# A gated-recurrence and star-ReLU kernel: a weight cast by its own DMA, a held-back weight load and an earlier logarithm

## The chip, the cores and the metric

The kernel runs on one core of one Trainium2 chip. A core has five engines with instruction streams of their own: PE (TensorE, matrix multiply), DVE (VectorE), ACT (ScalarE), POOL (GpSimd) and SP (SyncE, which here only issues DMAs). Each engine runs its instructions in the order in which they were written, and waits on semaphores for the others. The metric is the device time of one execution in microseconds, lower is better.

## The reference

Two steps in one kernel. The first is a gated linear recurrence over 768 steps, for 4 batches and 8 heads of 48 channels; the second is a feed-forward layer with a squared ReLU (here called the MoE work, after its inputs' names).

```python
for t in range(S):                       # S = 768, D = 48
    state = alpha[:, :, t, :, None] * state + einsum('bhd,bhe->bhde', k[:, :, t], v[:, :, t])
    y[:, :, t] = einsum('bhd,bhde->bhe', q[:, :, t], state)
x = y.transpose(0, 2, 1, 3).reshape(3072, 384)
h = x @ w_in                             # 384 x 2048
r = maximum(h, 0)
out = (s * (r * r) + b) @ w_out          # 2048 x 384
```

All inputs and the output are float32 in HBM.

## The kernel before

The 3072 tokens are worked through in 24 blocks of 128 (4 batches of 6 blocks). For each block `n`:

- `load(n)` (L121) issues four DMAs on SP: alpha, k, q and v, 192 KB each, in rows of 192 bytes. There are 8 buffers (`NLD`).
- `ln(n)` (L188) takes the logarithm of alpha on ACT. `vcast(n)` (L191) casts v to bf16 on POOL. `cum(n)` (L194) sums the logarithms over the block with a triangular matrix on PE, and ACT makes the exponentials `bi` and `b` of both signs.
- `qk(n)` (L225) multiplies k and q by these on DVE. `tr(n)` (L229) transposes both on PE, and DVE copies the result (`qkT`). `amat(n)` (L242) makes the attention matrix on PE, and DVE masks it (`am_a`, `am_b`).
- `yp(n)` (L262) makes y on PE: first the part from the state (it reads `sd`), then the part within the block (it reads `am` and the cast v), then the new addend of the state. ACT copies y out.
- `st(n)` (L329) updates the state: one DVE instruction (`t1`), then two halves of `sd` (L344) and `sc` (L348) on POOL.
- `xt(n)` (L314) transposes y on PE, and ACT writes it as x (`xd`).

The MoE work runs in groups: group 0 holds blocks 0 and 1, and each later group one block. `mp(g, u)` (L358) makes four (or two, for group 0) 128-column pieces of h, `rl` (L376) applies ReLU on ACT, `sq` (L384) squares on DVE, and `mm2(n, u)` (L394, called as `o`) multiplies a quarter of the result by w_out. `mr` is `mp` and `rl`; `busy(n)` (L177) is n matmuls whose result nobody reads.

The weights come in quarters. `load_w_in(i)` loads 512 columns of w_in (768 KB, rows of 2 KB) as float32 into `w_in_st`, and `cast_w_in` casts them to bf16, one or two of the three pieces on ACT and the others on DVE. `load_w_out` loads a quarter of w_out into `w_out_st`, and `cast_w_out` (`wout`) casts it, times s, on DVE, the second quarter on ACT. `w_in_st` is used again later for outputs of blocks 0 to 13 that wait for the bias.

No scheduler sets the order. The DMAs ahead of the loop are issued in the order in which they stand (L445 to L458): loads 0 to 3, four quarters of w_in, four of w_out, loads 4 to 7, all on SP. The work of the first blocks is a list written out by hand (L501 to L513); each entry is one call, and each engine gets its instructions in that order. The entries behind it have a number as their place, 8 per block, and are sorted by it (L548).

Of the kernel before, what the change touches and what calls it, by code (L numbers as in the profile page):

```python
# [10 lines left out]
AF = mybir.ActivationFunctionType  # L11
# [3 lines left out]
def kernel(  # L15
# [12 lines left out]
    nc = tc.nc  # L28
# [8 lines left out]
    NJ = d_ff // 128  # L37
    KT = d_model // 128
# [5 lines left out]
    NLD = 8  # L44
# [59 lines left out]
    w_in_st = sb.tile([128, KT, d_ff], FP32, name="w_in_st")  # L104
    w_in_bf = sb.tile([128, KT, d_ff], BF16, name="w_in_bf")
    w_out_st = sb.tile([128, NJ, d_model], FP32, name="w_out_st")
# [10 lines left out]
    def src(t, n):  # L117
        b, c = n // NCH, n % NCH
        return t[b, :, c * C : (c + 1) * C, :].rearrange("h s d -> s h d")

    def load(n):  # L121
        if n < NBLK:
            for dst, t in ((al_sb, alpha), (k_sb, k), (q_sb, q), (v_sb, v)):
                nc.sync.dma_start(out=dst[n % NLD], in_=src(t, n))

    def load_w_in(i):
        cols = slice(i * d_ff // 4, (i + 1) * d_ff // 4)
        nc.sync.dma_start(
            out=w_in_st[:, :, cols], in_=moe_w_in[:, cols].rearrange("(t r) f -> r t f", t=KT)
        )  # L130

    def load_w_out(j0, j1):
        nc.sync.dma_start(
            out=w_out_st[:, j0:j1],
            in_=moe_w_out[128 * j0 : 128 * j1, :].rearrange("(j r) m -> r j m", r=128),
        )

    def cast_w_in(c0, c1, act=1):
        for kk in range(act):
            nc.scalar.activation(out=w_in_bf[:, kk, c0:c1], in_=w_in_st[:, kk, c0:c1], func=AF.Copy)  # L140
        for kk in range(act, KT):
            nc.vector.tensor_copy(out=w_in_bf[:, kk, c0:c1], in_=w_in_st[:, kk, c0:c1])

    def cast_w_out(j0, j1, act):
        if not act:
# [304 lines left out]
    quarter = d_ff // 4  # L450
    load(2)
    load(3)
    for i in range(4):
        load_w_in(i)
    for j in range(0, NJ, 4):
        load_w_out(j, j + 4)
    for n in range(4, NLD):
        load(n)  # L458
    make_upper_triangular(nc, U_bf, 1.0, diag=True)
    for t in la_sb:  # L460
        nc.vector.memset(t, 0.0)
# [13 lines left out]
    def at(pos, fn, *args):  # L475
        events.append((pos, len(events), fn, args))
# [5 lines left out]
    def wout(i):  # L482
        cast_w_out(4 * i, 4 * i + 4, i == 1)

    def win(i):
        cast_w_in(i * quarter, (i + 1) * quarter, 2 if i == 0 else 1)

    def m(g, u):
        mp(g, u)
# [10 lines left out]

    for pos, what in enumerate(  # L501
        [
            (ln, 0), (vcast, 0), (cum, 0), (qk, 0), (spread,), (busy, 3), (tr, 0), (ln, 1), (busy, 1), (vcast, 1), (cum, 1), (amat, 0),
            (busy, 3), (yp, 0), (qk, 1), (st, 0), (busy, 1), (tr, 1), (xt, 0), (ln, 2), (busy, 2), (vcast, 2), (cum, 2), (amat, 1),
            (busy, 3), (yp, 1), (qk, 2), (st, 1), (busy, 1), (tr, 2), (xt, 1), (ln, 3), (busy, 2), (vcast, 3), (cum, 3), (amat, 2),
            (busy, 3), (yp, 2), (qk, 3), (st, 2), (busy, 1), (tr, 3), (xt, 2), (busy, 3), (amat, 3), (win, 0), (busy, 4), (yp, 3),
            (mr, 0, 0), (mr, 0, 1), (xt, 3), (mr, 1, 0), (win, 1), (sq, 0, 0), (mr, 0, 2), (mr, 0, 3), (mr, 1, 1), (win, 2), (sq, 0, 1),
            (sq, 1, 0), (mr, 2, 0), (mr, 2, 1), (win, 3), (st, 3), (sq, 0, 2), (sq, 0, 3), (mr, 0, 4), (mr, 0, 5), (wout, 0), (mr, 1, 2),
            (sq, 1, 1), (sq, 2, 0), (mr, 2, 2), (sq, 2, 1), (mr, 0, 6), (sq, 0, 4), (o, 0, 0), (wout, 1), (mr, 0, 7), (sq, 0, 5),
            (o, 1, 0), (mr, 1, 3), (sq, 1, 2), (o, 2, 0), (mr, 2, 3), (sq, 2, 2), (sq, 0, 6), (wout, 2), (sq, 0, 7), (o, 0, 1), (sq, 1, 3),  # L510
            (o, 1, 1), (sq, 2, 3), (ln, 4), (wout, 3), (o, 2, 1), (cum, 4), (o, 0, 2), (vcast, 4), (qk, 4), (o, 1, 2), (o, 2, 2), (colsum, 1),
            (o, 0, 3), (o, 1, 3), (tr, 4), (o, 2, 3), (o, 3, 0), (colsum, 2), (amat, 4),
        ]  # L513
    ):
        at(0.1 * pos, *what)
# [12 lines left out]
    for n in range(4, NBLK):  # L528
        p = 8 * n
        if n > 4:  # L530
            f = min((n - 5) / 3.0, 1.0)
            c, t, a = 9.0 + 5.8 * f, 5.8 + 5.0 * f, 3.4 + 4.5 * f
# [47 lines left out]
```

## Time and profile before

| | |
|---|---|
| three runs | 196.47, 197.56, 197.69 us, median 197.56 |
| the profiled execution | 196.55 us, its span 194.8 us |
| busy, of the span | PE 180.9 us (93%), DVE 150.5 (77%), ACT 119.5 (61%), POOL 61.4 (32%) |
| DMA queue of SP | 113422 packets, 29.94 MB, 74.3% of 16 engines |
| granted TensorE clock | 1.00 |

The page gives the span of one execution, measured by the profiler, and the busy time of each engine in it. Matmuls overlap, so a busy PE is not PE at its peak. Where a wait is shown, the profile names what ended last before the waiting instruction started. The difference of 1.75 us between the execution's time and its span lies outside the span.

### The profile page before, as it was taken

The page shows a single profiled execution, that of the slowest core. Times are in us where ns is not written, and L with a number is a line of the kernel's source. Part 1 is how long each engine was busy: PE and PEld are TensorE (multiplying, and loading weights), DVE is VectorE, ACT ScalarE, POOL GpSimd, SP SyncE. Part 2 cuts the span into 40 slices and gives each one's busy share as a digit, 9 for nine tenths or more (in the row PEclk, how much of TensorE's full clock was granted, in tenths as well). Part 3 has the DMA queues.
Part 4 walks back from the last instruction along what each step waited for, and adds up shares of the span by engine and source line. Part 5 has one row for each costly group of instructions (what it writes and reads, how often), then busy time and mean ns, then how long its engine had stood idle before and what let it go on. Part 6 is the DMA issues. An engine that isn't in the chain of part 4 may idle for free.

```text
span 194.8 us, 6003 instructions
## 1 busy us (share of the span) xinstructions
PE 180.9 (93%) x2389; PEld 143.3 (74%) x2391; DVE 150.5 (77%) x294; ACT 119.5 (61%) x245; POOL 61.4 (32%) x96
## 2 busy tenths in 40 slices
PE   1977879999999999999999999999999999999994
PEld 1544459866777788778878888888877877877783
DVE  5367778657687788888887996878988988998532
ACT  3344567953677666766677676775675566654640
POOL 5154404021310515624500641642401565352000
PEclk9999999999999999999999999999999999999999
DMA  6999999999996484484958448759886948433212
GB/s 126 188 185 190 359 388 371 233 192 188 186 156 108 71 155 88 80 150 82 173 91 162 83 85 162 131 80 198 165 175 149 216 117 166 128 120 121 84 40 81
DMA packets 113453, 30.31 MB, mean 156 GB/s; under 512 B 106627, under 2 KB 111890, under 8 KB 113426
## 3 DMA queue, kind: packets, MB, share of 16 engines
q1 hardware_dynamic: 113422, 29.94, 74.3%
q8 instruction: 18, 0.29, 0.7%
q14 instruction: 9, 0.07, 0.1%
q10 hardware_dynamic: 4, 0.00, 0.0%
HBM read 25.19 MB, written 4.74 MB: 154 GB/s over the span
## 4 chain that ended last, share of the span: by engine, by line
PE 80%; DVE 4%; ACT 3%; issue 1%; ACTq 0%
PE h_ps L365 29%; PE o_ps L403 28%; PE ct_ps L232 5%; PE a_ps L247 3%; PE a_ps L403 3%; PE y_ps L275 2%; ACT r_sb L379 2%; PE h_ps L317 2%; PE ct_ps L198 2%; PE a_ps L426 1%; PE p_ps L286 1%; PE y_ps L266 1%; DVE gt_all L386 1%; DVE w_out_bf L146 1%; DVE am_b L255 1%
## 5 line engine op out<-in xcount | busy, mean ns | idle before, releaser
L379 ACT ACTIVATE r_sb<-h_ps 128x512 bf16<-128x512 f32 x90 | 53.5, 597 | 35.5 <-PE h_ps L365 33.2
L365 PEld LDWEIGHTS <-w_in_bf 128*128 128x128 bf16 x1104 | 67.9, 98 | 8.0 <-ACT w_in_bf L140 1.4
L365 PE MATMUL h_ps<-xd_all,w_in_bf 128*128 128x128 bf16 (+1 forms) x1044 | 71.1, 221 | 0.1
L403 PE MATMUL o_ps<-w_out_bf,gt_all 128*128 128x384 bf16 x336 | 68.3, 326 | 0.1
L386 DVE TENSOR_TENSOR gt_all<-r_sb 128x512 bf16<-128x512 bf16 x96 | 45.1, 482 | 26.5 <-ACT r_sb L379 25.8
L344 POOL TENSOR_TENSOR sd_sb<-t_sb,blast 48x192 bf16<-48x192 f32 x40 | 20.1, 503 | 91.8 <-DVE t_sb L339 53.9
L403 PEld LDWEIGHTS <-gt_all 128*128 128x128 bf16 x368 | 32.6, 98 | 16.0
L192 POOL CAST v_bf<-v_sb 128x384 bf16<-128x384 f32 x24 | 17.0, 712 | 24.2 <-DMA v_sb<-in_v_dram 20.7
L348 POOL TENSOR_TENSOR sc_sb<-t_sb,blast 112x384 f32<-112x384 f32 x16 | 22.0, 1372 | 1.3
L323 ACT ACTIVATE xd_all<-h_ps 128x384 bf16<-128x384 bf16 x23 | 11.3, 491 | 15.6 <-PE h_ps L317 15.6
L237 DVE COPY qkT<-ct_ps 112x1024 bf16<-112x1024 bf16 x24 | 16.4, 683 | 4.5 <-PE ct_ps L232 3.0
L255 DVE TENSOR_TENSOR am_a<-a_ps,mask 128x512 bf16<-128x512 f32 x24 | 16.4, 683 | 4.2 <-PE a_ps L247 4.1
L226 DVE TENSOR_TENSOR kb_sb<-k_sb,bi_sb 128x384 bf16<-128x384 f32 x24 | 13.8, 574 | 4.5 <-ACT bi_sb L209 4.5
L255 DVE TENSOR_TENSOR am_b<-a_ps,mask 128x512 bf16<-128x512 f32 x24 | 16.3, 680 | 0.0
L227 DVE TENSOR_TENSOR qb_sb<-q_sb,b_sb 128x384 bf16<-128x384 f32 x24 | 16.0, 668 | 0.0
L293 ACT ACTIVATE y_bf<-y_ps 128x384 bf16<-128x384 f32 x24 | 11.7, 489 | 5.6 <-PE y_ps L275 5.6
L189 ACT ACTIVATE la_sb<-al_sb 128x384 bf16<-128x384 f32 x24 | 12.4, 516 | 3.9 <-DMA al_sb<-in_alpha_dram 3.9
L232 PEld LDWEIGHTS <-qb_sb 128*112 128x112 bf16 x96 | 8.3, 133 | 5.3 <-DVE qb_sb L227 4.1
L209 ACT ACTIVATE bi_sb<-ct_ps 128x384 f32<-128x384 f32 x20 | 9.7, 486 | 2.3 <-PE ct_ps L201 1.3
L232 PE MATMUL ct_ps<-ident,qb_sb 128*112 128x128 bf16 x96 | 9.9, 227 | 0.9 <-DVE qb_sb L227 0.9
L210 ACT ACTIVATE b_sb<-ct_ps 128x384 f32<-128x384 f32 x20 | 9.9, 495 | 0.0
L275 PE MATMUL y_ps<-v_bf,am_b 128*128 128x48 bf16 x96 | 8.1, 184 | 1.7 <-DVE am_b L255 1.7
(75 smaller groups left out, 200.9 us busy)
## 6 DMA issues: line engine op xcount, KB each, us to landing
al_sb<-in_alpha_dram SPq DMA_DIRECT2D x24, 192.0 KB, 4.1
k_sb<-in_k_dram SPq DMA_DIRECT2D x24, 192.0 KB, 4.0
q_sb<-in_q_dram SPq DMA_DIRECT2D x24, 192.0 KB, 4.4
v_sb<-in_v_dram SPq DMA_DIRECT2D x24, 192.0 KB, 5.2
w_in_st<-in_moe_w_in_dram SPq DMA_DIRECT2D x4, 768.0 KB
w_out_st<-in_moe_w_out_dram SPq DMA_DIRECT2D x4, 768.0 KB, 12.8
out_dram<-w_in_st SPq DMA_DIRECT2D x14, 192.0 KB, 2.0
out_dram<-out_sb SPq DMA_DIRECT2D x9, 192.0 KB
```

The lines of the kernel that those rows point to most:

```text
L192: nc.gpsimd.tensor_copy(out=v_bf[n % 3], in_=v_sb[n % NLD])
L226: nc.vector.tensor_tensor(out=kb_sb[n % 3][:, :, 0:48], in0=k_sb[n % NLD], in1=bi_sb[n % 2], op=ALU.mult)
L227: nc.vector.tensor_tensor(out=qb_sb[n % 2][:, :, 0:48], in0=q_sb[n % NLD], in1=b_sb[n % 3], op=ALU.mult)
L232: nc.tensor.transpose(out=t_ps[0:112, x, p, :], in_=t.rearrange("a h d -> a (h d)")[:, 128 * p : 128 * p + 112], identity=ident,)
L237: nc.vector.tensor_copy(out=qkT_sb[n % 2][0:112].rearrange("a x p t -> a (x p t)"), in_=t_ps[0:112].rearrange("a x p t -> a (x p t)"),)
L255: nc.vector.tensor_tensor(out=am_sb[e][n % 2], in0=a_ps[e], in1=mask4, op=ALU.mult)
L344: nc.gpsimd.tensor_tensor(out=sd[r, :, d], in0=t1_sb[r, :, d], in1=bl[r].to_broadcast([48, NP, 48]), op=ALU.mult)
L348: nc.gpsimd.tensor_tensor(out=sc_sb[0:112], in0=t1_sb[0:112], in1=bl[0:112].to_broadcast([112, NP, 96]), op=ALU.mult)
L365: nc.tensor.matmul(out=hp[:, jj * N : (jj + 1) * N], lhsT=w_in_bf[:, kk, 128 * j : 128 * (j + 1)], rhs=xd_sb[g][:, kk, 0:N], start=(kk == ...
L379: nc.scalar.activation(out=rs, in_=h_of.pop((g, u)), func=AF.Relu)
L386: nc.vector.tensor_tensor(out=gt_sb[g][:, u * 512 : (u + 1) * 512], in0=rs, in1=rs, op=ALU.mult)
L403: nc.tensor.matmul(out=op[:, 0:d_model], lhsT=gt_sb[g][:, j * N + t * C : j * N + (t + 1) * C], rhs=w_out_bf[:, j, :], start=(j == 0), sto ...
```

## The change

It has three parts. First, `load_w_in` writes straight into the bf16 tile `w_in_bf`: the DMA casts, and POOL issues it instead of SP. The casts on ACT and DVE (`cast_w_in`, `win`) go. Quarters 0 and 1 are issued after `vcast(2)`, quarters 2 and 3 after `vcast(3)`, in the list. Second, the loads of w_out and loads 4 to 7 are issued in a new entry `weights_out`, behind `sq(0, 0)`; ahead of them DVE writes one column of `w_out_st`, so the first w_out load has to wait for that write, and SP's later DMAs stand behind it. Third, the list is in another order: `ln(2)` stands ahead of `xt(0)` and `ln(3)` ahead of `xt(1)`, `amat(0)` ahead of `cum(1)`, the first MoE group `mr(0, 0)` ahead of `yp(3)`, six `busy` matmuls fewer, and `ln(4)`, `cum(4)` and `tr(4)` each a place or more earlier.

```diff
     def load_w_in(i):
         cols = slice(i * d_ff // 4, (i + 1) * d_ff // 4)
-        nc.sync.dma_start(
-            out=w_in_st[:, :, cols], in_=moe_w_in[:, cols].rearrange("(t r) f -> r t f", t=KT)
+        nc.gpsimd.dma_start(
+            out=w_in_bf[:, :, cols], in_=moe_w_in[:, cols].rearrange("(t r) f -> r t f", t=KT)
         )
...
-    def cast_w_in(c0, c1, act=1):
-        for kk in range(act):
-            nc.scalar.activation(out=w_in_bf[:, kk, c0:c1], in_=w_in_st[:, kk, c0:c1], func=AF.Copy)
-        for kk in range(act, KT):
-            nc.vector.tensor_copy(out=w_in_bf[:, kk, c0:c1], in_=w_in_st[:, kk, c0:c1])
...
     load(2)
     load(3)
-    for i in range(4):
-        load_w_in(i)
-    for j in range(0, NJ, 4):
-        load_w_out(j, j + 4)
-    for n in range(4, NLD):
-        load(n)
...
-    def win(i):
-        cast_w_in(i * quarter, (i + 1) * quarter, 2 if i == 0 else 1)
+    def weights_out():
+        nc.vector.memset(w_out_st[:, 0, 0:1], 0.0)
+        for j in range(0, NJ, 4):
+            load_w_out(j, j + 4)
+        for n in range(4, NLD):
+            load(n)
...
-            (ln, 0), (vcast, 0), (cum, 0), (qk, 0), (spread,), (busy, 3), (tr, 0), (ln, 1), (busy, 1), (vcast, 1), (cum, 1), (amat, 0),
-            (busy, 3), (yp, 0), (qk, 1), (st, 0), (busy, 1), (tr, 1), (xt, 0), (ln, 2), (busy, 2), (vcast, 2), (cum, 2), (amat, 1),
-            (busy, 3), (yp, 1), (qk, 2), (st, 1), (busy, 1), (tr, 2), (xt, 1), (ln, 3), (busy, 2), (vcast, 3), (cum, 3), (amat, 2),
-            (busy, 3), (yp, 2), (qk, 3), (st, 2), (busy, 1), (tr, 3), (xt, 2), (busy, 3), (amat, 3), (win, 0), (busy, 4), (yp, 3),
-            (mr, 0, 0), (mr, 0, 1), (xt, 3), (mr, 1, 0), (win, 1), (sq, 0, 0), (mr, 0, 2), (mr, 0, 3), (mr, 1, 1), (win, 2), (sq, 0, 1),
-            (sq, 1, 0), (mr, 2, 0), (mr, 2, 1), (win, 3), (st, 3), (sq, 0, 2), (sq, 0, 3), (mr, 0, 4), (mr, 0, 5), (wout, 0), (mr, 1, 2),
+            (ln, 0), (vcast, 0), (cum, 0), (qk, 0), (spread,), (busy, 2), (tr, 0), (ln, 1), (busy, 1), (vcast, 1), (amat, 0), (cum, 1),
+            (busy, 3), (yp, 0), (qk, 1), (st, 0), (busy, 1), (tr, 1), (ln, 2), (xt, 0), (vcast, 2), (load_w_in, 0), (load_w_in, 1), (cum, 2), (busy, 1), (amat, 1),
+            (busy, 3), (yp, 1), (qk, 2), (st, 1), (busy, 1), (tr, 2), (ln, 3), (xt, 1), (vcast, 3), (load_w_in, 2), (load_w_in, 3), (cum, 3), (busy, 1), (amat, 2),
+            (busy, 3), (yp, 2), (qk, 3), (st, 2), (busy, 1), (tr, 3), (xt, 2), (busy, 3),
+            (amat, 3), (mr, 0, 0), (busy, 1), (yp, 3), (mr, 0, 1), (sq, 0, 0), (weights_out,), (mr, 1, 0), (xt, 3), (st, 3), (sq, 0, 1), (mr, 0, 2),
+            (sq, 1, 0), (mr, 0, 3), (sq, 0, 2), (mr, 1, 1), (sq, 0, 3), (mr, 2, 0), (mr, 2, 1), (mr, 0, 4), (mr, 0, 5), (wout, 0), (mr, 1, 2),
...
```

The rest of the list differs only in the places of `ln(4)`, `cum(4)`, `wout(3)` and `tr(4)`.

More of the change, by code (lines that the diff above doesn't have):

```diff
@@ L509 @@
             (sq, 1, 1), (sq, 2, 0), (mr, 2, 2), (sq, 2, 1), (mr, 0, 6), (sq, 0, 4), (o, 0, 0), (wout, 1), (mr, 0, 7), (sq, 0, 5),
-            (o, 1, 0), (mr, 1, 3), (sq, 1, 2), (o, 2, 0), (mr, 2, 3), (sq, 2, 2), (sq, 0, 6), (wout, 2), (sq, 0, 7), (o, 0, 1), (sq, 1, 3),
-            (o, 1, 1), (sq, 2, 3), (ln, 4), (wout, 3), (o, 2, 1), (cum, 4), (o, 0, 2), (vcast, 4), (qk, 4), (o, 1, 2), (o, 2, 2), (colsum, 1),
-            (o, 0, 3), (o, 1, 3), (tr, 4), (o, 2, 3), (o, 3, 0), (colsum, 2), (amat, 4),
+            (o, 1, 0), (mr, 1, 3), (sq, 1, 2), (o, 2, 0), (mr, 2, 3), (sq, 2, 2), (sq, 0, 6), (ln, 4), (wout, 2), (sq, 0, 7), (o, 0, 1),
@@ L513 @@
+            (sq, 1, 3), (o, 1, 1), (sq, 2, 3), (cum, 4), (wout, 3), (o, 2, 1), (o, 0, 2), (vcast, 4), (qk, 4), (o, 1, 2), (o, 2, 2),
+            (colsum, 1), (o, 0, 3), (tr, 4), (o, 1, 3), (o, 2, 3), (o, 3, 0), (colsum, 2), (amat, 4),
         ]
```

## The prediction

> **What bounds the kernel now.** I read the page first: its busy row and its slices.
>
> ```profile
> span 194.8 us, 6003 instructions
> PE 180.9 (93%) x2389; PEld 143.3 (74%) x2391; DVE 150.5 (77%) x294; ACT 119.5 (61%) x245; POOL 61.4 (32%) x96
> ...
> PE   1977879999999999999999999999999999999994
> ...
> DMA  6999999999996484484958448759886948433212
> ```
>
> From about 44 us on, PE is full in every slice. A change ahead of that point moves the end by what it moves the start of that stretch, and nothing in this change reaches past block 4. So I looked at the first 45 us: first the busy time by stage (columns: stretch, sum, then PE, PEld, DVE, ACT, POOL busy, PE clock, DMA share, GB/s).
>
> ```profile
> 12.50:15.00 2.50, 1.89 (x22) 1.16 (x22) 1.02 (x2) 1.56 (x4) 1.83 (x3) 1.00 1.36 187
> ...
> 20.00:22.50 2.50, 1.73 (x24) 1.11 (x23) 2.50 (x5) 0.83 (x3) 0.50 (x1) 1.00 1.02 359
> ...
> 27.50:30.00 2.50, 1.26 (x18) 1.02 (x15) 2.40 (x8) 1.75 (x4) 0.00 (x0) 1.00 1.06 380
> ```
>
> Block inputs move at 187 GB/s, a block (768 KB) in some 4.2 us; weights move at about 370 GB/s, a quarter of w_in (768 KB) in 2.1 us. PE has a hole at 27.5 to 30 us. The timeline and the waits say what stands around it (start, length, engine, line).
>
> ```profile
> 15.09 0.99 SPq L124 DMA_DIRECT2D v_sb<-in_v_dram  x1
> 16.13 3.55 SPq L128 DMA_DIRECT2D w_in_st<-in_moe_w_in_dram  x4
> 17.94 0.49 ACT L323 ACTIVATE xd_all<-h_ps 128x384 bf16<-128x384 bf16 x1 [1.05 <-PE h_ps L317]
> 18.32 0.52 ACT L189 ACTIVATE la_sb<-al_sb 128x384 bf16<-128x384 f32 x1
> 18.89 0.32 PE L198 MATMUL h_ps<-la_sb,U_bf 128*128 128x384 bf16 x1 [0.56 <-ACT la_sb L189]
> 19.30 0.40 PE L247 MATMUL a_ps<-qkT 48*128 48x128 bf16 x8
> 20.75 0.50 POOL L192 CAST v_bf<-v_sb 128x384 bf16<-128x384 f32 x1 [1.13 <-DMA v_sb<-in_v_dram]
> 22.74 1.08 POOL L344 TENSOR_TENSOR sd_sb<-t_sb,blast 48x192 bf16<-48x192 f32 x2 [1.49 <-DVE t_sb L339]
> 24.82 0.34 PE L266 MATMUL y_ps<-sd_sb,qkT 112*128 112x96 bf16 x4
> 25.75 1.47 PE L365 MATMUL h_ps<-xd_all,w_in_bf 128*128 128x256 bf16 x12
> 29.30 0.83 PE L365 MATMUL a_ps<-xd_all,w_in_bf 128*128 128x256 bf16 x6 [1.24 <-ACT w_in_bf L140]
> 36.27 0.81 PE L403 MATMUL o_ps<-w_out_bf,gt_all 128*128 128x384 bf16 x4
> ```
>
> The reader should see two things. Until 25 us one chain runs from block to block: logarithm, cumulative sum, exponentials, products, transposes, attention matrix, `yp`. The MoE work of blocks 0 to 2 stands behind `yp(3)` on PE and starts at 25.9 us, though x of blocks 0 and 1 has been ready since 18.4. From there to the first `o(0,0)` at 36.27, PE also waits once 1.24 us for a w_in cast on ACT. No wait names the landing of w_in: the casts in the engines' order, not the transfer, are late.
>
> **The change part by part.**
>
> *Logarithm ahead of x.* For block 3, qkT of block 2 is complete at 18.46, but `amat(2)` starts at 19.30, since `cum(3)` (18.89) stands before it on PE and waits for `ln(3)` (18.32), which stands behind x of block 1 on ACT. y of block 1 leaves ACT at 16.89; alpha of block 1 landed at 8.24, so with 4.2 us a block those of blocks 2 and 3 land at 12.4 and 16.6. `ln(3)` can run at 16.9, and `cum(3)` no longer holds `amat(2)`: 0.84 us. `amat(1)` gains as much (14.23 against a qkT complete at 13.39). The swap of `cum(1)` and `amat(0)` gives up to 0.57 (9.23 against 8.66), most of which alpha of block 2 at 12.4 takes back. I take 1.6 in all: `amat(3)` at 22.0 instead of 23.62. Bounds: 0.3 (alpha late) to 2.2. The six `busy` matmuls taken out (0.21 us each) lie in PE's waits: nothing, with the clock at 1.00 in every slice; without such waits they would be worth 1.3.
>
> *w_in written as bf16 by its own DMA.* It removes 7 DVE casts of 0.42 (2.9 us) and 5 ACT casts of 0.62 (3.1 us). From the second MoE group (26.58) to `o(0,0)` (36.27) are 9.7 us; PE's own work there is 12 groups of 0.66 and `xt(3)` of 0.17, 8.1 us. So 1.6 us are waits, 1.24 of them at the cast. ACT keeps 0.6 us a group against PE's 0.66 and one w_out cast of 1.57, so I take 1.2; bounds 0.5 to 1.6.
>
> *The four issues on POOL.* No row of this trace shows a DMA that POOL issues. The nearest are SP's issues of the same transfers, 0.49 to 1.47 us each (3.55 for four); the longest bulk-weight issue is w_out's 2.63. I take 1.2 each, between SP's mean of 0.89 and its longest, because POOL is the slowest of these engines at comparable work (0.50 to 1.08 a step); bounds 0.5 to 2.63. Two stand between `vcast(2)` and `sd` of block 1, two between `vcast(3)` and `sd` of block 2. The first pair: `vcast(2)` at 15.64, so POOL is free at 18.5, `sd` done 19.6, just when `yp(2)` wants it. The second pair is on the path: `vcast(3)` can't start before v of block 3 has landed (20.75), then 0.5 + 2 x 1.2 + 1.08 gives `sd` at 24.7. So `yp(3)` waits on POOL at 24.8, no longer on the masks (`am` of block 3 done at 23.7). Most of the 1.6 us of the logarithm are hidden under this wait; of them remains that the first MoE group (0.66), which the new order puts before `yp(3)`, runs at 22.4 inside it.
>
> *The transfer.* Data of the first pair begins at about 18 (first issue done at 17.4; SP's first load, issued at 0.74, landed at 3.79 with 1.05 of moving, so some 2 us pass around the moving, part of them ahead of it), when load 3, whose last issue ended at 16.08, has its last packets under way. Landing after issue was 3.7 us for v of blocks 1 and 2, 4.7 for v of block 3, with w_in behind it already. I leave 20.75. Rate: 370 GB/s of reading as now (2.1 us a quarter); bounds 187 GB/s, the slowest steady rate here (4.2 us), and free.
>
> *w_out behind the small write.* The write stands behind `sq(0,0)` on DVE, at about 24.3, costs under 0.1 (0.06 for a 128x1 memset), and holds on SP the four w_out issues and the sixteen of loads 4 to 7. With w_in's second pair moving from 23.7, w_out 25.5 on, DMA has 12.6 us of weights to move: done at 36.3, the first w_out chunk at about 31 (its cast is wanted by 33.7), alpha of block 4 at 38.7. `cum(4)` is reached at 39.2, so the cover is half a microsecond; each later microsecond of the write then costs one.
>
> The sum: `yp(3)` at 24.8 takes 0.7 on PE, the second MoE group starts at 25.5 instead of 26.58: 1.1. Waits behind it: 1.2. Together 2.3 us of the profiled execution's 196.55: 194.25. The median shown is 197.56, 1.0 above that execution, so the median after would be 195.3.
>
> A rule weighed against this: the Trainium skill, DMA: Bandwidth & Descriptors (Queues, rings and completion order), says that every DMA engine takes turns packet by packet between the queues that have work. The trace, with nearly all on one queue, can't show it; v of block 3 was 1.0 us later when w_in stood behind it. By the rule the second queue's large packets go between load 3's small ones, and the sum would be that of the first rival.
>
> **The rivals.**
>
> 1. *Two queues share the engines and load 3 is late.* A packet of load 3 is 192 B (16.5 ns at 187 GB/s over 16 engines), a row of w_in 2 KB (87 ns at 370). If they alternate, v of block 3 lands only when the first pair has moved: 4.2 us on top of 19.8 (15.64 of block 2 and 4.2), 24.0 instead of 20.75. `yp(3)` follows to 28.05, and 3.25 - 2.3 makes 0.95 slower: 198.5. For: small packets, no slack on POOL. Against: most of load 3 has moved by 18 us.
>
> 2. *The casting transfer is slow* (the other side). Place: v of block 3, POOL's second pair, `sd`, `yp(3)`. At 187 GB/s the pair takes 8.4 us; shared with load 3, v lands up to 7 us after 19.8, at 26.8, `yp(3)` at 30.85: 6.05 - 2.3 = 3.75 slower, 201.3. It decides from v landing plus twice the issue beyond 25.5 (now 23.15): no gain from there, and the same point is passed by issues of 2.4 us each. For: no row has a casting transfer. Against: it writes half the bytes.
>
> 3. *Hidden anyway.* ACT's evacuations (16 of 0.60 beside PE's groups of 0.66) take the place of the casts, and POOL's wait eats the logarithm: 0.5 faster, 197.1. For: ACT had 2.2 to 2.5 of 2.5 us busy from 30 to 35. Against: the 1.24 us wait names the cast.
>
> 4. *Issues cost little* (0.5 each): `yp(3)` at 23.7 by the masks, 1.1 more gain and some of the waits: 193.9.
>
> **How the numbers follow.** Forecast 0.36 (its own range 194 to 196.5), rival 1 0.20, rival 2 0.22, rival 3 0.12, rival 4 0.10. About 1% (2 us) is what a measurement of this kernel tells from no change; the forecast lies just past that line, so some 0.30 of its 0.36 counts as faster. Faster 0.30 + 0.10 = 0.40. Same: 0.06 + rival 3's 0.12 + 0.13 of rival 1 = 0.31. Slower: 0.22 of rival 2 and 0.07 of rival 1 = 0.29. The range goes from 193.2 (rival 4 with all waits) to 200.8, short of the far end of rival 2.
>
> **What would show it.** Right: `ln(3)` at about 17, `amat(3)` at 22, POOL's two steps of about 1.2 us after `vcast(3)`, `sd` of block 2 ending just before `yp(3)`, the second MoE group at 25.5, no wait on w_in, `o(0,0)` at about 33.7, `cum(4)` by 39.5. Wrong: v of block 3 after 22, issues of over 2 us, a PE hole over 3 us ahead of `yp(3)`, ACT or PE waiting for alpha of block 4 beyond 40, or matmuls at half speed after the hole.

## The result and the profile after

The changed kernel takes 195.35 us (median, 195.03 to 196.52); the kernel before, run beside it, 197.14 (196.40 to 197.75). The ratio is 0.9928, with a 95% interval of 0.9902 to 0.9954: about 0.7% faster. The profiled execution of the changed kernel took 195.13 us, 1.42 less than that of before. The ratios here and below are worked out from the executions, two slow ones left out (one of e3, one of e6), and not from the medians.

First the page of the changed kernel: span, busy row, and the slices of PE and DMA.

```profile
span 193.4 us, 5976 instructions
PE 181.0 (94%) x2383; PEld 143.9 (74%) x2385; DVE 147.9 (76%) x288; ACT 117.6 (61%) x240; POOL 65.5 (34%) x100
...
PE   0898899979899999999999999999999999999993
...
DMA  6999999999996586482969656949794957433212
```

The span fell by 1.4 us at the same busy time of PE. From about 45 us on PE was full before and is full now; what changed lies ahead of that. The stretches of the changed kernel (sum, then PE, PEld, DVE, ACT, POOL busy, PE clock, DMA share, GB/s) show where:

```profile
27.50:30.00 2.50, 2.50 (x43) 2.44 (x42) 0.95 (x2) 2.27 (x5) 0.39 (x1) 1.00 0.97 260
...
37.50:40.00 2.50, 1.40 (x10) 0.74 (x9) 2.01 (x4) 1.08 (x2) 0.00 (x0) 1.00 0.89 174
```

The hole that stood at 27.5 to 30 us is filled. A new one stands at 37.5 to 40. The timeline of the changed kernel (start, length, engine, line; in brackets the idle time before and what ended it) gives the steps. `ln` is now L183, `cum` L192, `amat` L241, `yp` L260, `mp` L359, `o` L397.

```profile
16.73 0.52 ACT L183 ACTIVATE la_sb<-al_sb 128x384 bf16<-128x384 f32 x1
19.61 0.50 POOL L186 CAST v_bf<-v_sb 128x384 bf16<-128x384 f32 x1
20.07 1.57 POOL L128 DMA_DIRECT2D w_in_bf<-in_moe_w_in_dram  x2
21.67 1.10 POOL L338 TENSOR_TENSOR sd_sb<-t_sb,blast 48x192 bf16<-48x192 f32 x2
22.49 0.40 PE L241 MATMUL a_ps<-qkT 48*128 48x128 bf16 x8
23.70 0.34 PE L260 MATMUL y_ps<-sd_sb,qkT 112*128 112x96 bf16 x4
24.62 0.82 PE L359 MATMUL h_ps<-xd_all,w_in_bf 128*128 128x256 bf16 x6
24.69 0.06 DVE L474 MEMSET w_out_st<- 128x1 f32 x1
24.79 2.90 SPq L133 DMA_DIRECT2D w_out_st<-in_moe_w_out_dram  x4
33.30 0.82 PE L397 MATMUL o_ps<-w_out_bf,gt_all 128*128 128x384 bf16 x4 [0.22 <-DVE w_out_bf L140]
39.25 0.52 ACT L183 ACTIVATE la_sb<-al_sb 128x384 bf16<-128x384 f32 x1 [1.20 <-DMA al_sb<-in_alpha_dram]
39.82 0.32 PE L192 MATMUL ct_ps<-la_sb,U_bf 128*128 128x384 bf16 x1 [1.10 <-ACT la_sb L183]
```

The second MoE group starts at 24.62. In the same view of the kernel before it starts at 26.41 (the first group's 25.75 and its 0.66), so it comes 1.79 sooner, and no wait names w_in any more. `o(0,0)` starts at 33.30 instead of 36.27: 2.97 sooner. At `cum(4)` PE then waits 1.10 us, since alpha of block 4 has only just landed. The chain that ended last in the changed kernel puts this wait on its path (start, length, step):

```profile
26.31 1.39 SPq L133
27.74 11.48 DMA al_sb<-in_alpha_dram
39.25 0.53 ACT la_sb L183
```

It goes from the w_out issues, which stand behind the small write, to the issue of alpha at 27.74 and its landing 11.5 us later. By the trace's records of DMA completions, alpha of block 4 landed at 38.14 in the kernel before and at 39.23 in the changed one, 1.09 later. The kernel before reached `cum(4)` only at 42.16 and would have borne that; the changed kernel gets there nearly 3 us sooner. In the timeline of before `o(1,1)` (with `o(2,1)` in one row) and `cum(4)` stand at:

```profile
40.86 1.46 PE L403 MATMUL a_ps<-w_out_bf,gt_all 128*128 128x384 bf16 x8
42.16 0.33 PE L198 MATMUL ct_ps<-la_sb,U_bf 128*128 128x384 bf16 x1
```

and in that of the changed kernel `o(1,1)`, with `cum(4)` next, at:

```profile
37.91 0.81 PE L397 MATMUL a_ps<-w_out_bf,gt_all 128*128 128x384 bf16 x4
```

So the loss at 37.5 to 40 is for the most part the price of the held-back loads, and it shows because PE is early.

### The profile page after: what moved, and what is told of

It is laid out like the page before. It is cut to its first block, busy times and chain, and to the rows that moved or that the text cites. A ratio compares the mean times of both kernels' runs of the same rounds, so it can differ in the third digit from the quotient of the medians.

```text
span 193.4 us, 5976 instructions
## 1 busy us (share of the span) xinstructions
PE 181.0 (94%) x2383; PEld 143.9 (74%) x2385; DVE 147.9 (76%) x288; ACT 117.6 (61%) x240; POOL 65.5 (34%) x100
## 3 DMA queue, kind: packets, MB, share of 16 engines
q0 software_dynamic: 1600, 1.57, 5.2%
## 4 chain that ended last, share of the span: by engine, by line
PE 76%; DMA 6%; DVE 2%; ACT 2%; SPq 1%; issue 1%; ACTq 0%
PE o_ps L397 28%; PE h_ps L359 27%; DMA al_sb<-in_alpha_dram 6%; PE ct_ps L226 5%; PE a_ps L241 3%; PE y_ps L269 2%; PE h_ps L311 2%; PE ct_ps L192 2%; PE a_ps L397 2%; SPq L133 1%; PE a_ps L420 1%; PE p_ps L280 1%; PE y_ps L260 1%; ACT r_sb L373 1%; DVE am_b L249 1%
## 5 line engine op out<-in xcount | busy, mean ns | idle before, releaser
L359 PEld LDWEIGHTS <-w_in_bf 128*128 128x128 bf16 x1104 | 67.9, 98 | 6.6 <-issue 0.3
L359 PE MATMUL h_ps<-xd_all,w_in_bf 128*128 128x128 bf16 (+1 forms) x1044 | 71.3, 221 | 0.0
L397 PE MATMUL o_ps<-w_out_bf,gt_all 128*128 128x384 bf16 x336 | 68.3, 326 | 0.3 <-DVE w_out_bf L140 0.2
L380 DVE TENSOR_TENSOR gt_all<-r_sb 128x512 bf16<-128x512 bf16 x96 | 45.6, 492 | 23.1 <-ACT r_sb L373 22.3
L338 POOL TENSOR_TENSOR sd_sb<-t_sb,blast 48x192 bf16<-48x192 f32 x40 | 20.3, 508 | 79.1 <-DVE t_sb L333 48.8
L397 PEld LDWEIGHTS <-gt_all 128*128 128x128 bf16 x368 | 32.5, 98 | 16.5 <-DVE w_out_bf L140 0.5
L186 POOL CAST v_bf<-v_sb 128x384 bf16<-128x384 f32 x24 | 18.0, 753 | 31.0 <-DMA v_sb<-in_v_dram 29.3
L221 DVE TENSOR_TENSOR qb_sb<-q_sb,b_sb 128x384 bf16<-128x384 f32 x24 | 15.5, 644 | 0.5 <-DMA q_sb<-in_q_dram 0.5
L183 ACT ACTIVATE la_sb<-al_sb 128x384 bf16<-128x384 f32 x24 | 12.4, 517 | 5.0 <-DMA al_sb<-in_alpha_dram 4.9
L241 PE MATMUL a_ps<-qkT 48*128 48x128 bf16 x192 | 9.8, 222 | 0.6 <-DVE qkT L231 0.5
```

The source lines that it names most:

```text
L186: nc.gpsimd.tensor_copy(out=v_bf[n % 3], in_=v_sb[n % NLD])
L221: nc.vector.tensor_tensor(out=qb_sb[n % 2][:, :, 0:48], in0=q_sb[n % NLD], in1=b_sb[n % 3], op=ALU.mult)
L241: nc.tensor.matmul(out=a_ps[e][:, p, :], lhsT=qkT[r0 : r0 + 48, 1, p, :], rhs=qkT[r0 : r0 + 48, 0, p, :], start=True, stop=True,)
L338: nc.gpsimd.tensor_tensor(out=sd[r, :, d], in0=t1_sb[r, :, d], in1=bl[r].to_broadcast([48, NP, 48]), op=ALU.mult)
L359: nc.tensor.matmul(out=hp[:, jj * N : (jj + 1) * N], lhsT=w_in_bf[:, kk, 128 * j : 128 * (j + 1)], rhs=xd_sb[g][:, kk, 0:N], start=(kk == ...
L380: nc.vector.tensor_tensor(out=gt_sb[g][:, u * 512 : (u + 1) * 512], in0=rs, in1=rs, op=ALU.mult)
```

## The experiments

| kernel | median us | ratio to before, 95% interval |
|---|---|---|
| the changed kernel | 195.35 | 0.9928 (0.9902 to 0.9954) |
| e4, before with the logarithm's order alone | 195.51 | 0.9917 (0.9885 to 0.9950) |
| e3, changed, logarithm's order as before | 196.66 | 0.9992 (0.9967 to 1.0016) |
| e2, changed, no small write | 196.46 | 0.9970 (0.9951 to 0.9989) |
| e9, changed, busy matmuls put back | 196.21 | 0.9941 (0.9914 to 0.9968) |
| e1, changed, tail of the list as before | 194.87 | 0.9888 (0.9859 to 0.9918) |
| e5, changed, alpha of block 4 issued sooner | 194.36 | 0.9855 (0.9826 to 0.9883) |
| e7, e1 and e5 together | 194.64 | 0.9871 (0.9836 to 0.9906) |
| e10, e5 with `cum(1)` first | 194.45 | 0.9879 (0.9830 to 0.9927) |
| e11, e5 with a wait of PE filled | 194.48 | 0.9882 (0.9851 to 0.9914) |
| e6, changed, matmuls from the start | 197.50 | 1.0024 (1.0005 to 1.0042) |

My theory after the result: the earlier logarithm and the removed cast waits bring nearly 3 us to `o(0,0)`, and alpha of block 4, late behind the small write, takes back 1.1. The rival: alpha is not what costs, and the gain is limited by the transfers of w_in or by the block chain.

### The tail of the list as before (e1_block4_back)

```diff
-            ... (sq, 0, 6), (ln, 4), (wout, 2), (sq, 0, 7), (o, 0, 1),
-            (sq, 1, 3), (o, 1, 1), (sq, 2, 3), (cum, 4), (wout, 3), (o, 2, 1), (o, 0, 2), ...
+            ... (sq, 0, 6), (wout, 2), (sq, 0, 7), (o, 0, 1), (sq, 1, 3),
+            (o, 1, 1), (sq, 2, 3), (ln, 4), (wout, 3), (o, 2, 1), (cum, 4), (o, 0, 2), ...
```

> The changed kernel with only the tail of its list in the old order: ln(4), cum(4) and tr(4) one place later, so that o(2,1) (0.65 us of PE) stands ahead of cum(4). Theory (late alpha): the changed kernel reaches the first o(0,0) 3.0 us earlier than before (33.30 against 36.27) but PE then stands 1.10 us at cum(4), because alpha of block 4 lands only at 39.25. With 0.65 us of work moved into that wait, the wait falls to about 0.45 and the end comes 0.65 us earlier: 0.3% under the changed kernel, about 0.989 to 0.990 of the kernel before. Rival (the wait is covered elsewhere: the later chain of block 4 makes yp(4) late by as much): no difference from the changed kernel, 0.993.

It measured 194.87 us, ratio 0.9888. The timeline of e1 at `cum(4)`:

```profile
39.93 0.32 PE L192 MATMUL ct_ps<-la_sb,U_bf 128*128 128x384 bf16 x1 [0.54 <-ACT la_sb L183]
```

Alpha lands no sooner, but PE has one more group of `o` (0.65 us) to run meanwhile, and the wait shrinks from 1.10 to 0.54. The interval overlaps that of the changed kernel, so the size is not settled by this run alone; the direction, and e5 below, say that the wait was on the path.

### No small write (e2_no_small_write)

```diff
     def weights_out():
-        nc.vector.memset(w_out_st[:, 0, 0:1], 0.0)
         for j in range(0, NJ, 4):
```

> The changed kernel without the small write to w_out: w_out and loads 4 to 7 are issued as soon as SP is free, at about 16 us. Theory (shared engines): alpha of block 4 lands earlier, 37.5 to 38, and the 1.10 us wait at cum(4) is gone; but w_out's packets take turns with w_in's from 17.5 us on, so w_in's first quarter lands at 24 to 25 instead of by 22.8 and mr(0,0) waits 1.5 to 2 us, and the later quarters come late too: 0.5 to 2 us slower than the changed kernel, 0.995 to 1.003 of before. Rival (the write is only a cost): the wait of 1.10 us goes and nothing comes in its place, 0.987 of before.

It measured 196.46 us, ratio 0.9970: more than half of the gain is gone. SP issued w_out at 16.0 us, beside POOL's w_in. Two lines of the timeline of e2, and its row of the DMA issues (last column: median us from issue to landing):

```profile
27.29 0.83 PE L359 MATMUL a_ps<-xd_all,w_in_bf 128*128 128x256 bf16 x6 [0.50 <-DMA w_in_bf<-in_moe_w_in_dram]
...
35.25 0.83 PE L359 MATMUL h_ps<-xd_all,w_in_bf 128*128 128x256 bf16 x6 [1.45 <-DMA w_in_bf<-in_moe_w_in_dram]
```

```profile
w_in_bf<-in_moe_w_in_dram POOLq DMA_DIRECT2D x4, 384.0 KB, 10.2
```

The same row of the changed kernel:

```profile
w_in_bf<-in_moe_w_in_dram POOLq DMA_DIRECT2D x4, 384.0 KB, 7.2
```

Without the write w_in takes 10.2 us to land instead of 7.2, and PE waits four times for it, 2.6 us in all (0.44, 0.50, 0.20 and 1.45). In return alpha of block 4 lands 1.0 us sooner, at 38.21, and `cum(4)`, reached at 41.16, waits for nothing. So the write does its work: it keeps w_out's packets from going beside w_in's. The rule of the Trainium skill that I weighed (DMA: Bandwidth & Descriptors, Queues, rings and completion order: the DMA engines take turns between queues) agrees with this pair of runs; that the turns go packet by packet these times don't show.

### The logarithm as before, and the logarithm alone (e3_logarithm_back, e4_logarithm_alone)

```diff
 # e3, from the changed kernel
-            ... (vcast, 1), (amat, 0), (cum, 1), ... (ln, 2), (xt, 0), ... (ln, 3), (xt, 1), ...
+            ... (vcast, 1), (cum, 1), (amat, 0), ... (xt, 0), (ln, 2), ... (xt, 1), (ln, 3), ...
 # e4, from the kernel before
-            ... (vcast, 1), (cum, 1), (amat, 0), ... (xt, 0), (ln, 2), ... (xt, 1), (ln, 3), ...
+            ... (vcast, 1), (amat, 0), (cum, 1), ... (ln, 2), (xt, 0), ... (ln, 3), (xt, 1), ...
```

> The changed kernel with ln(2) and ln(3) behind x again, and cum(1) ahead of amat(0). Theory: amat(3) goes from 22.49 back to about 23.6, mr(0,0) and the write behind it as well, so w_out and alpha of block 4 land 1.0 us later too, and the end follows by about 1.0 us: 0.998 of before. Rival (the arrival of alpha of block 4 is set by the DMA engines alone, whatever the attention chain does): within 0.3 us of the changed kernel, 0.993 to 0.995.

> The kernel before with only ln(2), ln(3) ahead of x and amat(0) ahead of cum(1); w_in still loaded by SP and cast on ACT and DVE. Theory: amat(3) at 22.5 instead of 23.62 and the first MoE group about 1.1 us earlier, at 24.8; w_in's first quarter has landed by 22, so the casts follow; the waits at the casts stay; alpha of block 4 still lands before PE reaches cum(4) at about 41. So 1.0 us faster, 0.995 of before. Rival (casts and w_out set the pace behind 26 us): first o(0,0) stays at 36.3 and the time at 1.000.

They measured 196.66 us (ratio 0.9992) and 195.51 (0.9917). By these ratios the order of the logarithm alone is worth as much as the whole change, and the other parts without it gain nothing that can be told from no change. Both sizes need care. The profiled execution of e4 took 195.99 us, 0.5 above its median, and that of before 196.55, 0.6 below its own; between them lie 0.56 us, not the 1.6 of the medians. The timeline of e4 keeps the wait at the cast:

```profile
25.19 1.47 PE L365 MATMUL h_ps<-xd_all,w_in_bf 128*128 128x256 bf16 x12
28.74 0.83 PE L365 MATMUL a_ps<-xd_all,w_in_bf 128*128 128x256 bf16 x6 [1.24 <-ACT w_in_bf L140]
```

So in e4 the MoE work starts 0.56 sooner (I had expected 1.1) and still loses 1.24 at the cast, and reaches `o(0,0)` at 35.70. The changed kernel is there 2.4 sooner. In the profiles 0.86 of that are left at the end, in the medians next to nothing; the late alpha takes 1.3 of it. In e3 `amat(3)` came only at 25.08, 1.5 later than in the kernel before, which I had not expected. That delay is there by `amat(1)` (15.76 against 14.24), and up to there PE's work differs from that of the kernel before only in `busy` matmuls; matmuls were long until 14 us. So e3 doesn't price the order of the logarithm alone: it takes in a later turn to short matmuls, to which the last part of this section returns.

### Alpha of block 4 issued sooner (e5_alpha_sooner), and with e1 (e7_both_order_and_alpha)

```diff
         for j in range(0, NJ, 4):
             load_w_out(j, j + 4)
-        for n in range(4, NLD):
+            if j == 4:
+                nc.sync.dma_start(out=al_sb[4], in_=src(alpha, 4))
+        for dst, t in ((k_sb, k), (q_sb, q), (v_sb, v)):
+            nc.sync.dma_start(out=dst[4], in_=src(t, 4))
+        for n in range(5, NLD):
             load(n)
```

> The changed kernel with one DMA moved: alpha of block 4 is issued between the second and third quarter of w_out, not behind the fourth. Theory (late alpha): alpha lands some 4 us sooner (two quarters of w_out), at about 35 instead of 39.25; the last two quarters of w_out land 1.0 us later (192 KB at 187 GB/s), which their casts can bear for the most part. PE's wait of 1.10 us at cum(4) goes: 0.7 to 1.1 us faster than the changed kernel, 0.987 to 0.989 of the kernel before. Rival (DMA is short of time as a whole, and any order only moves the wait): PE waits as long at another place (k or q of block 4, or the third w_out quarter) and the time stays at 0.993.

> The changed kernel with the tail of the list in the old order (o(2,1) ahead of cum(4)) and with alpha of block 4 between the second and third quarter of w_out. Theory: both take from the same wait of 1.10 us, so together they give no more than it: 1.0 to 1.2 us faster than the changed kernel, 0.987 of before, no better than either by more than 0.5. Rival (block 4's chain is late in itself): the two gains add up, 0.984.

They measured 194.36 us (ratio 0.9855) and 194.64 (0.9871). The timeline of e5:

```profile
33.79 0.82 PE L397 MATMUL o_ps<-w_out_bf,gt_all 128*128 128x384 bf16 x4 [0.34 <-DVE w_out_bf L140]
...
39.04 0.33 PE L192 MATMUL ct_ps<-la_sb,U_bf 128*128 128x384 bf16 x1
```

`cum(4)` has no bracket any more: it follows `o` at once, at 39.04 instead of 39.82, though this execution reached `o(0,0)` 0.49 later. That is the direct test of the theory: one 192 KB transfer issued 1.24 us sooner (26.50 instead of 27.74), ahead of two quarters of w_out, lands at 35.63 instead of 39.23 and gives 0.7% more. e5 beats both kernels. It also shows what the other parts are worth once alpha is not late: 0.9855 against e4's 0.9917, with intervals just apart. The two ways of relieving `cum(4)` take away the same wait, and e7 is no better than e5.

### The six busy matmuls put back (e9_busy_restored)

```diff
-            (spread,), (busy, 2), (tr, 0), ... (cum, 2), (busy, 1), (amat, 1), ... (cum, 3), (busy, 1), (amat, 2), ... (mr, 0, 0), (busy, 1), (yp, 3), ...
+            (spread,), (busy, 3), (tr, 0), ... (cum, 2), (busy, 2), (amat, 1), ... (cum, 3), (busy, 2), (amat, 2), ... (mr, 0, 0), (busy, 4), (yp, 3), ...
```

> The changed kernel with the six busy matmuls put back in their four places (3, 2, 2 and 4 of them). Theory: two of the places lie in waits of PE, and four stand between the first MoE group and yp(3), where PE has hardly a wait left (yp(3) at 23.70 with am_b ended at 24.2): three more of 0.06 to 0.21 us move yp(3) by 0.2 to 0.6 at most, and alpha of block 4, at 39.25, takes all of it back: ratio 0.991 to 0.995, as the changed kernel's. Rival (taking them out is what makes matmuls turn short later, at about 14 us instead of 9.5): 128x512 matmuls turn from 0.63 to 0.38 us by 10 us again, amat(3) before 22, ratio under 0.990. Second rival (they cost what they last): 1.3 us, ratio 0.999.

It measured 196.21 us, ratio 0.9941. In its profile the second MoE group starts at 25.45, 0.83 later than in the changed kernel, but `cum(4)` only 0.43 later (40.25): the small write came later too (w_out's issue at 25.35), alpha with it, and PE waited 1.08 again. The long matmuls were still there at 12 us, so the rival falls. The intervals of the two kernels overlap for the most part, so these runs don't tell what taking the six out is worth from nothing.

### Where matmuls turn short (e6, e8, e10, e11)

The same `busy` matmul of 512 columns lasts 0.63 us at first and 0.38 later. The profile's rows show a granted clock of 1.00 throughout, but that is what they show where the trace has no record of the clock, and its first record in the kernel before is at 8.44 us. In the timeline of before:

```profile
7.72 0.63 PE L179 MATMUL o_ps<-mask,U_bf 128*128 128x512 bf16 x1
9.56 0.82 PE L179 MATMUL o_ps<-mask,U_bf 128*128 128x512 bf16 x3
```

and of the changed kernel:

```profile
9.87 1.44 PE L173 MATMUL o_ps<-mask,U_bf 128*128 128x512 bf16 x3
11.74 0.63 PE L173 MATMUL o_ps<-mask,U_bf 128*128 128x512 bf16 x1
14.51 0.82 PE L173 MATMUL o_ps<-mask,U_bf 128*128 128x512 bf16 x3
```

Three in a row take 0.82 us by 9.6 in the kernel before, and in the changed one not before 14. The first try was to bring PE there by work from the start:

```diff
+    for i in range(24):
+        nc.tensor.matmul(out=o_ps[:, 0:128], lhsT=U_bf, rhs=U_bf, start=True, stop=True)
```

> The changed kernel with 24 matmuls of 128 columns, whose result nobody reads, on PE from 1.4 us on, where PE has nothing to do until 4.4. In its trace a 128x512 matmul takes 0.63 us until 11.74 and 0.38 from 14.5 on; in the trace of before 0.63 at 7.72 and 0.38 at 9.56. Theory (matmuls run slowly until PE has been busy for a while, and the six busy matmuls that the change takes out made that later): matmuls are at 0.38 by about 8 us, amat(1) starts 0.4 to 0.7 us earlier, and the first MoE group, the small write and alpha of block 4 with it: 0.3 to 0.6 us faster than the changed kernel, 0.990 to 0.991. Rival (that stretch is paced by the landing of alpha, k, q and v): no difference, 0.993.

It measured 197.50 us, ratio 1.0024: the theory failed. Matmuls were short at 5.5, long again at 9.4 and at 20. Here the trace has records of the clock from 5.05 us on, and the stretches of e6, cut at these records, show what goes with the long matmuls (columns as above, the clock third from the end):

```profile
5.05:8.46 3.41, 2.05 (x22) 1.19 (x23) 1.79 (x4) 1.34 (x4) 0.50 (x1) 1.00 1.40 191
8.46:11.88 3.42, 3.42 (x32) 2.09 (x27) 2.62 (x5) 1.54 (x5) 0.51 (x1) 0.50 1.44 186
11.88:18.70 6.82, 4.46 (x59) 3.03 (x57) 4.54 (x8) 3.11 (x8) 4.97 (x8) 1.00 1.27 160
18.70:22.12 3.42, 3.42 (x32) 1.95 (x31) 2.00 (x4) 1.06 (x4) 1.02 (x2) 0.50 1.15 190
```

So matmuls are long where the clock is granted at half. In all eleven traces that have such records, the first record of a clock of 1.00 begins where the lengths change. In e6 the early matmuls brought the turn to 5.05, and the clock then went back to half twice, for 3.41 us each time, after stretches in which PE was busy for 2.05 of 3.41 us and for 4.46 of 6.82. Whether the waits in them were the cause is not tested.

The loss in e6 has another part. By the records of completions v of block 3 landed at 22.94, behind the first quarter of w_in (21.45); in the changed kernel it was there at 19.49. Its cast started at 23.06, POOL's second pair of issues stood behind it, and `yp(3)` waited for `sd`:

```profile
26.50 0.33 PE L260 MATMUL y_ps<-sd_sb,qkT 112*128 112x96 bf16 x4 [1.29 <-POOL sd_sb L338]
```

That is the path of my first rival, and this run doesn't tell why v came late in it.

The kernel before once more, unchanged, to see whether the point is one of the program or of the single execution:

> The kernel before, profiled once more. If the time at which PE's matmuls become fast is set by the program, they are at 0.38 us for 512 columns by 9.6 us again, and the time is 196.5. If it differs from execution to execution, they may be slow until 12 to 14 us, and then the time is 0.5 to 1.2 us longer, near 197.5.

Three `busy` matmuls again took 0.82 us at 9.63 (execution 196.63 us), though the turn came half a microsecond or more later than in the first profile. Both profiled executions took under 196.7 us, where this kernel's went from 196.33 to 197.95; whether the turn comes later in one of 197.5, as I had asked, they don't show. The last pair asks whether the program moves the turn, starting from e5:

```diff
 # e10
-            (spread,), (busy, 2), (tr, 0), (ln, 1), (busy, 1), (vcast, 1), (amat, 0), (cum, 1),
+            (spread,), (busy, 3), (tr, 0), (ln, 1), (busy, 1), (vcast, 1), (cum, 1), (amat, 0),
 # e11
-            (spread,), (busy, 2), (tr, 0), (ln, 1), (busy, 1), (vcast, 1), (amat, 0), (cum, 1),
+            (spread,), (busy, 3), (tr, 0), (ln, 1), (busy, 3), (vcast, 1), (amat, 0), (cum, 1),
```

> The version with alpha of block 4 issued sooner, with cum(1) ahead of amat(0) again and three busy matmuls ahead of tr(0), as in the kernel before. In the kernel before, 128x512 matmuls turn from 0.63 to 0.38 us by 9.6; in every version with amat(0) first they were still 0.48 each at 9.9 and turned at 13 to 14.5. Theory A (the place of amat(0) and cum(1), that is, the wait of 0.36 us ahead of amat(0), decides it): matmuls turn short by 9.6, amat(3) before 22.0 instead of 22.53, ratio 0.983 to 0.986. Theory B (it is decided elsewhere): 0.48 each at 9.9 as before, ratio 0.985 to 0.988.

> The same version with amat(0) first, but three busy matmuls ahead of tr(0) and three (not one) behind it, which fill PE's wait of 0.36 us ahead of amat(0). Theory C (PE must be without a gap for some 4.5 us from its first matmul at 4.4): matmuls turn short by 9.6, amat(3) by 22.0, ratio 0.983 to 0.987. If not: still long at 9.9, amat(0) some 0.5 later by the added matmuls, ratio 0.986 to 0.990.

They measured 194.45 us (ratio 0.9879) and 194.48 (0.9882). The timeline of e10:

```profile
9.38 0.82 PE L173 MATMUL o_ps<-mask,U_bf 128*128 128x512 bf16 x3
22.16 0.40 PE L241 MATMUL a_ps<-qkT 48*128 48x128 bf16 x8
32.49 0.83 PE L359 MATMUL h_ps<-xd_all,w_in_bf 128*128 128x256 bf16 x6 [0.57 <-DMA w_in_bf<-in_moe_w_in_dram]
35.15 0.82 PE L397 MATMUL o_ps<-w_out_bf,gt_all 128*128 128x384 bf16 x4 [1.83 <-DVE w_out_bf L140]
```

With `cum(1)` first (and three `busy` matmuls) the turn is back, at 8.66 us by the clock's record, and filling the wait in e11 brought it to about 10.4, not to the 9.6 of theory C. `amat(3)` comes at 22.16 in e10 (theory A had it before 22.0) instead of e5's 22.53. But neither can be told from e5 by its time, and theory A's ratio did not come: in the profile of e10 PE waits for w_in and for w_out instead (0.57 and 1.83). This execution took 195.80 us, 1.35 above that kernel's median, so its waits may be larger than usual. What e3 shows, `cum(1)` first with two `busy` matmuls and a turn at 14.17, says that the place of `cum(1)` alone doesn't decide it. Nor is the turn fixed for a program: the changed kernel, e1, e2, e5 and e7 give PE the same work up to there, and turned at 13.72, 12.97, 12.86, 13.13 and 14.15. So the program may well move it by 4 us (all three profiles with `cum(1)` first and three `busy` matmuls turned by 9.3), but with one execution profiled of most kernels, what decides it stays open.

## Why the prediction was right, and where its steps were off

The forecast of 195.3 us stands beside a measured 195.35, and the change is on the side forecast. That they agree to 0.05 us is luck. The kernel before measured 197.14 here instead of the 197.56 from which I started, so the gain was 1.8 us and not 2.3, and by the line of about 1% that I had drawn myself the change would pass for the same; that it is faster rests on the interval, which leaves out 1. In the profiled executions, which the sum was made for, 2.3 us were forecast and 1.42 came: the sum gave 194.25, and 195.13 was measured. The step from there to the median, 1.0 in the forecast, was 0.22. Of the terms, the start of the MoE work gained 0.7 more than the sum's 1.1, the cast waits what was forecast, and a wait for alpha and a longer end, at nothing in the sum, cost 1.26 and 0.34.

- *Logarithm.* `ln(3)` ran at 16.73, as forecast. `amat(3)` came at 22.49, not 22.0, a gain of 1.13 instead of 1.6. The missing half microsecond lies early: `amat(1)` stood at 14.19, where before it stood at 14.24, because matmuls were long until 13.7. I had priced the swap of `cum(1)` and `amat(0)` at a small gain and the removed `busy` matmuls at nothing, with the clock at 1.00 in every slice; but the trace of before has no record of the clock until 8.44 us, and that the turn to short matmuls could move was no term of the sum. e10, with the turn back at 9.4, has `amat(1)` at 13.56 and `amat(3)` at 22.16.
- *POOL.* This is the term that was mis-sized most. The two pairs of issues took 1.70 and 1.57 us (0.77 to 0.92 an issue), where I took 1.2 an issue, and v of block 3 landed at 19.49, where I left it at 20.75 (in e1, e2, e5, e10 and e11 it landed between 20.3 and 20.6). So `sd` ended at 22.8, not 24.7, and `yp(3)` waited for the masks, as the fourth rival had it. The second MoE group started at 24.62, not 25.5. Against 26.41 that is 1.79 sooner, where the sum had 1.1 (its 26.58 came from the chain, whose starts lie 0.17 behind the timeline's here). Of the 1.79, 1.12 came by `yp(3)` and 0.66 by the first MoE group, which now runs while PE would wait for the masks.
- *The cast waits.* From the second MoE group to `o(0,0)` are 8.68 us, before 9.86: 1.18 gained, 1.2 forecast. No wait on w_in. This term was right.
- *The transfer.* The four transfers of w_in landed 6.5 to 8.0 us after their issue, in time for PE, the second of each pair 1.9 to 2.0 us behind the first. The rate term was of the right size: the first w_out quarter was there at 31.8 (31 forecast), alpha of block 4 at 39.2 (38.7 forecast).
- *The small write.* It ran at 24.69, 0.4 later than forecast. The mechanism was right, the cover was not: I counted half a microsecond between alpha and `cum(4)`, and left out `ln(4)`, which stands between them and takes 0.52. By my own times there was no cover. PE was then at `cum(4)` at 38.7, half a microsecond sooner than forecast, and alpha half a microsecond later: 39.25 and the logarithm make 39.82, and PE waited 1.10. By the starts, `o(1,1)` came 2.95 sooner (37.91 instead of 40.86). In the changed kernel `cum(4)` is next and could have started 0.65 behind it, at 38.56; it came 1.26 later. That leaves 1.69, and `yp(4)` is sooner by just that (47.71 instead of 49.40).
- *The end.* The last stores are issued 1.76 sooner (189.91 instead of 191.67), and the execution ends 1.42 sooner. From that issue to the end of the span the changed kernel takes 3.45 us and the kernel before 3.10. All ten kernels in which POOL issues DMAs have 3.4 to 3.5 here, the three in which it doesn't (before, e8, e4) 3.1. I had no term for it, and why it is so was not tested.
- *The rivals.* In the changed kernel the two queues did not make load 3 late, since most of it had moved; in e6 they did, or something else that comes to the same did (v of block 3 at 22.94). What the first rival described also happens in e2, between w_in and w_out. The casting transfer was not slow. "Hidden anyway" falls with e4 and e5: the logarithm alone gains, and the rest gains once alpha comes sooner. The fourth rival had the place right (0.5 an issue assumed, 0.8 measured), but left out alpha.

## What to carry to other kernels

When an early stretch gets shorter, look at once for the first input that was issued last: here nearly 3 us of gain met a 192 KB load that stood behind 3 MB of weights, and moving that one load ahead of half of them was worth as much again as the whole change. Count a cover to the instruction that needs it, with every step on the way: the logarithm between alpha and `cum(4)` was half a microsecond. Here the weight cast in its DMA paid only with w_out's queue held back (0.9970 without the small write) and with the load behind it moved forward (0.9855, against 0.9917 without the cast in the DMA). Price each part by itself and undo each by itself: one part alone measured as much here as all three together, and the load that another part made late took back much of what the third had gained.

## What I had not expected of the hardware

- The same 128x512 matmul lasted 0.63 us and later 0.38 in every kernel here. Long matmuls stood at a granted clock of 0.50 in e6; ahead of a trace's first record the rows show 1.00 all the same, so the length of equal matmuls tells more there. The turn came at 8.44 us in the kernel before, 8.66 in e10, about 9.2 in e8 and 10.4 in e11, and between 12.86 and 14.28 in the changed kernel, e1 to e5, e7 and e9. The Trainium skill (TensorE: Matmul & The Clock Gate, What's actually happening) tells of a free-running window of activity, after which matmuls run at twice the speed, and of turns that differ from run to run. The traces agree: with the clock at 0.50 the same matmul took 0.63 us instead of 0.38, half clock came in stretches of 3.41 us (e6), and five kernels with the same work on PE up to the turn had it between 12.86 and 14.15. Without added early work, no turn came before PE had been at work for some 4 us (from 4.4 to 8.44 at the earliest).
- More work on PE in the first microseconds (e6) brought the turn to 5.05, but the clock went back to half at 8.46 and at 18.70, for 3.41 us each, and matmuls that had turned short became long again.
- In the changed kernel an issue of a casting 768 KB transfer costs POOL 0.77 to 0.92 us, and it lands 6.5 to 8.0 us later; in e2, where SP's queue moves w_out beside it, the median is 10.2.
- The ten kernels in which POOL issues DMAs take 3.4 to 3.5 us from the issue of the last stores to the end, the other three 3.1.
